# Transnormer attention and bilinear feed-forward on one core: batch 2's load ahead of w_out, batch 1's attention ahead of block 0's feed-forward, block 0's output product in pieces of two matmuls

## The chip, the cores and the metric

The kernel runs on one core of a Trainium2 chip. The metric is the device time of one execution in microseconds (us), the median of several runs. Profiles come from one profiled execution; their clock starts with the span, so a "time" in the text is the number of microseconds after the span's start. PE is the matrix engine (TensorE), DVE is VectorE, ACT is ScalarE, POOL is GpSimd and SP is SyncE. POOL and SP are used here to issue DMA transfers, ACT for a few.

## The reference

There are two parts, one after the other. The first is linear attention without a softmax, for 8 batches of 8 heads, 576 positions and a head width of 64. The second is a bilinear feed-forward on all 4608 tokens, with width 512 and inner width 1536.

```python
kv  = einsum('bhsd,bhse->bhde', k, v)            # 64 x 64 for each head
o   = einsum('bhsd,bhde->bhse', q, kv)
o   = o / sqrt(mean(o*o, axis=-1) + 1e-6) * g_norm
x   = o.transpose(0, 2, 1, 3).reshape(4608, 512) # heads side by side
out = ((x @ w_a) * (x @ w_b)) @ w_out
```

All inputs and the output are float32 in memory. The kernel casts to bf16 (attention) and f16 (feed-forward) as it loads.

## The kernel before, in words

**Attention.** The eight heads of a batch are handled as four pairs p, the 576 positions as two halves h of 288. For each of the eight (p, h) a chain runs: a PE product with the pair's kv matrix (`x_mm`, L344), ACT squares it (`sq_op`, L354), a PE product with a block of ones sums the squares (`s_mm`, L358), ACT makes the reciprocal root (`rs_op`, L362), and DVE scales the product by g and that root and writes it as f16 into `xp` (`xt_op`, L367), already transposed, as the right-hand side of the feed-forward. Both products of a chain take banks of a pool of three PSUM banks (rings `RQ` and `RS`, two each).

Batches 0 and 1 are loaded "early" with positions on partitions; PE transposes their q (L332) and makes their kv products in small matmuls (L316). They lie in tiles that are used for other things later (`abt`, `u`, `as`, `so`, `o_sb`, `c`, `T`). Batches 2 to 7 are loaded by `load_node`: POOL issues a copy of q into a scratch in DRAM (L562, two DMAs), k (L568, L569, five) and v (L574, L578, two), then SP issues one DMA that transposes the scratch into `qT` (L583). Their kv product is one group of 20 matmuls (L529). A load waits for the transpose of the load before it (`gate_t`, L559). k, v and qT have two buffers each.

**Feed-forward.** Tokens go in nine blocks of 512. Block 0 is done plainly (`std_block`, L378): for each of the 12 f-chunks, four matmuls with w_a and four with w_b, ACT copies the first result (L389) and DVE multiplies it by the second (L393) into `abt`. Its output product (`o_std`, L830) is four groups of 12 matmuls with w_out, ACT copies (L845), SP stores (L801).

Blocks 1 to 8 use Strassen's scheme in Winograd's form, with seven products in place of eight. Their x differences are four DVE operations for a block (L698), and each of six units j makes seven products of four matmuls of 256 columns (`wino_block`, L729). These are p1, p2, p6, p5, p7, p4 and p3, of which p1, p6, p7 and p4 accumulate in one bank X, with an ACT copy to `u` or `c` (L411) after each; p2 has a bank Y, and p5 and p3 share a bank Z. Three DVE additions (c11, c22, c12; L748) and one product (L783) end a unit. The weights need sums and differences of their own, made once by DVE: `weight_sums` (L638 of `four`, 16 operations, which can only change a weight in place when block 0 has read it) and `out_sums` for w_out (four operations, after block 0's output product has read it). The output product of blocks 1 to 8 is `o_unit` (L894), with DVE sums (L879), ACT copies (L926) and DVE additions (L932) and stores (L801); that of the last block is cut finer and uses two more banks W, so that the p4 products have banks of their own.

**What sets the order.** All operations are nodes of a `Plan`. Each has an engine, a duration, a priority number (lower goes first), dependencies and buffers that it takes and frees. `Plan.order()` simulates the engines and gives one fixed order; instructions are issued in that order on each engine, and semaphores keep the data right. Times of arrival of loaded data are written into it as constants (`W_AT`, `EARLY_AT`, `plan.at(46.5)` for w_out, and `issue_us`, `q_us`, `kv_us` in `load_node`). Priorities are times too: `at_win[b]` is the window over which a batch's attention is spread, `st[i]` the start of block i, `o_win` the window of an output product. The nodes of `load_node` go to POOL and SP; the early DMAs, with all weights, are issued before the plan's first node, in the order of the code. So the DMAs on POOL are: early batch 0, seven pieces of w_a and w_b each with batch 1's two halves between them, w_out in two halves (L296), and then batch 2 and the rest.

Of the kernel before, what the change touches and what calls it, by code (L numbers as in the profile page):

```python
# [135 lines left out]
def kernel(  # L136
# [11 lines left out]
    nc = tc.nc  # L148

    B, H, S, D = q.shape  # L150
    d_model = H * D
# [3 lines left out]
    FC = d_ff // 128  # L155
# [12 lines left out]
        [(5.2, 5.2, 6.0), (6.4, 7.0, 8.0), (7.6, 8.4, 9.2), (10.0, 10.8, 11.7)],  # L168
        [(19.0, 20.5, 22.0)] * 2 + [(28.8, 30.3, 31.8)] * 2,
    ]  # L170
    HP = H // 2
    R = 4 * S
    HM = d_ff // 2
# [2 lines left out]
    NMAX = N0 // 2  # L176
    nb = len(BLOCKS)
    NJ = FC // 2
    EH = d_model // 2

    const = ctx.enter_context(tc.tile_pool(name="const", bufs=1))
# [11 lines left out]
    wo_t = sb("wo_t", [128, FC, d_model], FP16)  # L193
# [53 lines left out]
    for p, homes in ((0, "woo"), (1, "ppc")):  # L247
        for n, src, eng, home in zip("qkv", (q, k, v), (nc.scalar, nc.sync, nc.sync), homes):
            t = carve(home, 2 * EC * D, FP32)[0:EP].rearrange("p (h c d) -> p h c d", h=2, d=D)
# [20 lines left out]
    for i in range(2):  # L270
        t = const.tile([128, NP, 128], BF16, name=f"kvd{i}")
# [14 lines left out]
    wo_v = moe_w_out.rearrange("(fc p) e -> p fc e", p=128)  # L286

    for i, (f0, f1) in enumerate(WB):
        sl = slice(f0, f1)
        nc.gpsimd.dma_start(out=wa_t[:, :, sl], in_=wa_v[:, :, sl])  # L290
        nc.gpsimd.dma_start(out=wb_t[:, :, sl], in_=wb_v[:, :, sl])
        if i in (2, 4):
            early_load(early[1], 1, slice((i // 2 - 1) * HP, i // 2 * HP))
    for i in range(2):
        sl = slice(i * FC // 2, (i + 1) * FC // 2)
        nc.gpsimd.dma_start(out=wo_t[:, sl, :], in_=wo_v[:, sl, :])  # L296


    def dummies(n):
# [97 lines left out]
    def mm_us(n, cols):  # L397
        return n * (cols / 2400 + 0.0025)
# [16 lines left out]
    plan = Plan({"PE": 5.7, "DVE": 3.3, "ACT": 2.7, "SP": 5.0, "POOL": 22.5, "V": 0.0})  # L415
# [96 lines left out]
    def late_batch(b, load, win):  # L512
        at = Attn(b)
        w0, w1 = win
        kb, vb, qb = load["k"], load["v"], load["q"]
        kd = Buf(RKD)
        at.qt = [qb, kd]

        def view(t):
            return t[:, 0 : H * (NCH + 1) * D].rearrange("p (h c d) -> p h c d", h=H, d=D)  # L520

        s = Buf(RS)

        def kv_mm():
            kv_ps = s.tile[:].rearrange("p (a e) -> p a e", a=NP)
            for c in range(NCH + 1):
                for p in range(NP):
                    hs = slice(2 * p, 2 * p + 2)
                    nc.tensor.matmul(  # L529
                        kv_ps[:, p, :],  # L530
                        lhsT=kb.tile[:, c, hs, :],
                        rhs=view(vb.tile)[:, hs, c, :],
                        start=(c == 0 and p == 0),
                        stop=(c == NCH and p == NP - 1),
                    )

        n = plan.add(
            "PE", 1.15, w0, kv_mm, [(load["n"], load["kv_us"]), plan.at(w0 - 3)], [s, kd], [kb, vb]
        )

        def kv_out():
            kv_ps = s.tile[:].rearrange("p (a e) -> p a e", a=NP)
            at.kvd = kd.tile
            nc.scalar.copy(at.kvd[0:D, :, 0:D], kv_ps[0:D, :, 0:D])
            nc.scalar.copy(at.kvd[D:, :, D:], kv_ps[D:, :, D:])
            for p in range(NP):
                at.q[p] = qb.tile[:, p, :]

        m = plan.add("ACT", 0.75, w0, kv_out, [n], (), [s])
        slices(at, (w0 + 0.12 * (w1 - w0), w1), lambda p: [m, (load["qn"], 5.5)])  # L550


    def load_node(b, prio, dep):
        ld = {"k": Buf(RK), "v": Buf(RV), "q": Buf(RQT)}
        scr = scr_pool.tile([NP, S, 2, D], BF16, name="scr", tag="scr")

        def issue():
            if dep is not None:
                nc.gpsimd.tensor_copy(gate_t, dep["q"].tile[0:1, 0, 0:1])  # L559
            qv = q[b].rearrange("(p hl) s d -> hl s p d", hl=2)  # L560
            for hl in range(2):
                nc.gpsimd.dma_start(  # L562
                    out=scr[:, :, hl, :].rearrange("p s d -> s p d"), in_=qv[hl]
                )
            kt = ld["k"].tile
            ks = k[b, :, 0:SA, :].rearrange("h (sp c) d -> sp h c d", c=NCH)
            for c in range(NCH):
                nc.gpsimd.dma_start(out=kt[:, c], in_=ks[:, :, c, :])  # L568
            nc.gpsimd.dma_start(out=kt[0:SB, NCH], in_=k[b, :, SA:S, :].rearrange("h sp d -> sp h d"))  # L569
            for n, src in (("v", v),):  # L570
                t = ld[n].tile[:, 0 : H * (NCH + 1) * D].rearrange(
                    "p (h c d) -> p h c d", h=H, d=D
                )
                nc.gpsimd.dma_start(  # L574
                    out=t[:, :, 0:NCH, :],
                    in_=src[b, :, 0:SA, :].rearrange("h (sp c) d -> sp h c d", c=NCH),
                )
                nc.gpsimd.dma_start(  # L578
                    out=t[0:SB, :, NCH, :], in_=src[b, :, SA:S, :].rearrange("h sp d -> sp h d")
                )  # L580

        def transpose():
            nc.sync.dma_start_transpose(  # L583
                out=ld["q"].tile[:].rearrange("p a s -> p (a s)"),
                in_=scr[:].rearrange("a s h d -> (a s) (h d)"),
            )

        issue_us, q_us, ld["kv_us"] = (18.0, 8.0, 18.0) if dep is None else (9.0, 1.5, 11.5)

        ld["n"] = plan.add(  # L590
            "POOL", issue_us, prio, issue, [(dep["qn"], 5.5)] if dep else [], [ld["k"], ld["v"]]
        )
        ld["qn"] = plan.add(
            "SP", 2.5, prio, transpose, [(ld["n"], q_us)], [ld["q"]]
        )
        return ld
# [70 lines left out]
    def out_sums(prio):  # L667
        add, sub = nc.vector.tensor_add, nc.vector.tensor_sub
        b11, b12 = wo_t[:, 0:NJ, 0:EH], wo_t[:, 0:NJ, EH:]
        b21, b22 = wo_t[:, NJ:, 0:EH], wo_t[:, NJ:, EH:]  # L670
        t2, t3, t4 = (so_t[:, i] for i in range(3))
        n3, n1, n2, n4 = four(
            prio,
            fast_us(NJ * EH),
            ((t3, b22, b12, sub), (b12, b12, b11, sub), (t2, b22, b12, sub), (t4, b21, t2, sub)),
            [plan.at(46.5)],
            list(o_reads),
        )
        return n1, n2, n3, n4
# [140 lines left out]
    def o_std(ab, muls, win):  # L820
        w0, w1 = win
        ob = Buf(ROS)
        ng, copied = N0 // 128, []
        for g in range(ng):
            pr = w0 + (w1 - w0) * g / ng
            ps = Buf((RO, RY)[g % 2])

            def mm(g=g, ps=ps):
                for fc in range(FC):
                    nc.tensor.matmul(  # L830
                        ps.tile[:],
                        lhsT=ab.tile[:, fc, g * 128 : (g + 1) * 128],
                        rhs=wo_t[:, fc, :],
                        start=(fc == 0),
                        stop=(fc == FC - 1),
                    )

            n1 = plan.add(
                "PE", mm_us(FC, d_model), pr, mm,
                [plan.at(46.5)] + list(muls.values()), [ps], [ab],  # L840
            )
            o_reads.append(n1)
            n2 = plan.add(
                "ACT", act_us(d_model), pr,
                lambda g=g, ps=ps: nc.scalar.copy(ob.tile[:, g], ps.tile[:]),  # L845
                [n1] + copied[-1:], [ob] if g == 0 else [], [ps],
            )
            copied.append(n2)
            plan.add(
                "SP", 0.45, pr + 1, lambda g=g: store(g * 128, ob.tile[:, g]), [n2], (), [ob]  # L850
            )

    def o_unit(r0, ab, muls, osum, pr, du, chunks, pieces, m, w, first, second, X, Y, Z, ob, s2, s3, s4, W):
        v = nc.vector
# [95 lines left out]
        n1, n2, n3, n4 = osum  # L950
        if W:
# [22 lines left out]
                c21 = comb(6 + 0.1 * i, 1, 0, W[i], [p4, e3], [W[i]], subs)  # L974
                put(1, subs, [c21, c22], queue=("ACT", "SP")[i])
            return
        p1 = prod(0, X, a11, b11, True, [plan.at(46.5)], [X])
        e1 = ev(0, 0, 0, p1, [ob])
        p2 = prod(1, Y, a12, b21, True, [], [Y])
        c11 = comb(1, 0, 0, Y, [p2, e1], [Y])  # L980
# [17 lines left out]
    st = [T0]  # L998
    for i in range(len(lens)):
        st.append(st[-1] + lens[i] + (o_us[i - 1] if i else 0) + late_us * n_at[i])  # L1000
    L = [st[i + 1] - st[i] for i in range(len(lens))]
    at_win = {1: (34.5, st[1] - 3)}
    for b in range(2, B):
        t = b * S / N0
        at_win[b] = (max(61.0, st[int(t) - 1] + (t % 1) * L[int(t) - 1] - 18), st[int(t)] - 22 + (t % 1) * 12)
    loads = {2: load_node(2, 22.5, None)}
    for b in range(3, B):
        loads[b] = load_node(b, at_win[b - 1][0], loads[b - 1])
    early_batch(0, (4.0, 16.0))
    early_batch(1, at_win[1])  # L1010
    ab, muls, reads = std_block((st[0], st[1]))
    wsum = weight_sums(32.5, reads)
    needs = {1: [], 2: [2], 3: [3], 4: [4], 5: [5], 6: [6], 7: [7], 8: []}
    O_A, O_B = 12.0, 3.0
    for bi in range(1, nb + 1):
        o_win = (st[bi] + 1.0, st[bi + 1] - 1.0) if bi < nb else (st[bi] + O_A, st[bi + 1] + O_B)
        if bi == 1:
            o_std(ab, muls, o_win)
            osum = out_sums(st[2] - 10)
        else:  # L1020
            o_block(bi - 1, ab, muls, osum, o_win, 2, (RO, RY, RY), 1)
        for b in needs[bi]:
            late_batch(b, loads[b], at_win[b])
        ab, muls = wino_block(bi, (st[bi], st[bi + 1]), wsum)
# [40 lines left out]
```

## Time and profile before

| | |
|---|---|
| median of 5 runs | 306.39 us (306.2 to 307.17) |
| profiled execution, its own time | 306.52 us |
| its span, first to last instruction | 304.7 us |
| mean granted PE clock | 0.987 |
| PE busy | 292.1 us, 96% of the span |
| DVE busy | 234.8 us, 77% |
| ACT busy | 192.9 us, 63% |
| POOL busy | 76.3 us, 25% |

The profiled execution has 1.8 us outside its span. Matmuls overlap in the profile: a matmul of 256 columns is shown as 273 ns long while the next starts 109 ns later, so PE's "busy" share is no measure of lost time, and the starts are the thing to read. The page's second part cuts the span into 40 slices of 7.6 us, with one digit for a tenth of busy time. In a timeline a row gives start, length, engine, line, operation, what is written from what, the shape, how many are merged, and in brackets the idle time before it and what ended it. A row of the waits gives who waited for whom, the total, the number of waits and the longest.

### The profile page before, as it was taken

To read this page: it belongs to the slowest core of one execution; us is meant where nothing else is said; L and a number is where in the kernel's file an instruction comes from. 1 tells how busy PE (TensorE), PEld (TensorE's weight loads), DVE (VectorE), ACT (ScalarE), POOL (GpSimd) and SP (SyncE) were. 2 spreads that over 40 slices of the span, in tenths; PEclk is the share of its full clock that TensorE was granted. 3 is DMA by queue.
4 is the path that set the end of the run, shared out by engine and by line. 5 is a ranking of instruction groups with operands and counts; after the bars stand their busy time and mean duration, and the time that the engine had idled before them with its cause. 6 is when DMAs were issued, how large, how long until landed. Compare 5 with 4: busy or idle time off the path is not lost.

```text
span 304.7 us, 6666 instructions
## 1 busy us (share of the span) xinstructions
PE 292.1 (96%) x2620; PEld 239.1 (78%) x2621; DVE 234.8 (77%) x433; ACT 192.9 (63%) x404; POOL 76.3 (25%) x93
## 2 busy tenths in 40 slices
PE   7699899999999999999999999999999999999992
PEld 2444445498788898888988898889888888888881
DVE  4343778569998979698969986998599849898652
ACT  3574456289897768875688548965797466655520
POOL 8665742092470831904700000000000000000000
PEclk9699999999999999999999999999999999999999
DMA  8999999999799899999964400030004001100123
GB/s 197 209 199 198 199 205 159 187 180 170 78 144 160 55 156 242 114 175 168 155 73 80 138 3 0 2 140 1 2 0 140 1 2 69 72 3 0 51 89 138
DMA packets 98815, 33.16 MB, mean 109 GB/s; under 512 B 76768, under 2 KB 94176, under 8 KB 98784
## 3 DMA queue, kind: packets, MB, share of 16 engines
q0 software_dynamic: 77984, 17.99, 63.2%
q1 hardware_dynamic: 20096, 13.64, 18.5%
q10 hardware_dynamic: 704, 1.11, 1.2%
q8 instruction: 20, 0.33, 0.4%
q14 instruction: 11, 0.09, 0.1%
HBM read 37.75 MB, written 12.98 MB: 166 GB/s over the span
## 4 chain that ended last, share of the span: by engine, by line
PE 90%; DVE 4%; DMA 3%; ACT 1%; SPq 0%; issue 0%; DVEq 0%
PE bk L729 47%; PE bk L894 24%; PE bk L378 7%; PE bk L830 3%; DMA c<-in_v_dram 3%; PE bk L358 3%; PE bk L344 2%; PE bk L529 2%; PE bk L316 1%; DVE c L748 1%; DVE o_sb L932 1%; PE bk L332 1%; ACT rs L362 0%; DVE abt L393 0%; DVE xp L367 0%; SPq L250 0%
## 5 line engine op out<-in xcount | busy, mean ns | idle before, releaser
L748 DVE TENSOR_TENSOR c<-bk,u 128x512 f16<-128x512 f32 x144 | 96.6, 685 | 27.2 <-PE bk L729 13.2
L411 ACT COPY u<-bk 128x512 f32<-128x512 f32 x144 | 82.2, 591 | 37.5 <-PE bk L729 36.4
L729 PE MATMUL bk<-xp,wa_t 128*128 128x256 f16 x288 | 55.0, 273 | 0.0
L729 PE MATMUL bk<-xp,wb_t 128*128 128x256 f16 x288 | 55.0, 273 | 0.0
L729 PEld LDWEIGHTS <-wa_t 128*128 128x128 f16 x384 | 37.4, 98 | 5.1
L367 DVE SCALAR_TENSOR_TENSOR xp<-bk,g_col,rs 128x288 f16<-128x288 f32 x64 | 32.5, 511 | 11.4 <-ACT rs L362 11.2
L894 PEld LDWEIGHTS <-abt 128*128 128x128 f16 x384 | 37.5, 98 | 4.8 <-DVE abt L783 0.2
L729 PEld LDWEIGHTS <-wb_t 128*128 128x128 f16 x384 | 37.6, 98 | 4.4
L411 ACT CAST c<-bk 128x512 f16<-128x512 f32 x48 | 28.3, 590 | 17.2 <-PE bk L729 16.6
L894 PE MATMUL bk<-wo_t,abt 128*128 128x256 f16 x288 | 37.0, 273 | 0.0
L729 PE MATMUL bk<-T,sa 128*128 128x256 f16 x192 | 36.6, 273 | 0.1
L729 PE MATMUL bk<-T,sb 128*128 128x256 f16 x192 | 36.6, 273 | 0.0
L362 ACT ACTIVATE rs<-bk,eps_t 128x288 f32<-128x288 f32 x64 | 32.4, 508 | 3.5 <-PE bk L358 3.2
L783 DVE TENSOR_TENSOR abt<-c 128x1024 f16<-128x1024 f16 x48 | 32.9, 685 | 1.7
L729 PEld LDWEIGHTS <-sa 128*128 128x128 f16 x288 | 28.1, 98 | 4.4 <-issue 0.7
L894 PEld LDWEIGHTS <-as 128*128 128x128 f16 x288 | 28.2, 98 | 3.4
L729 PEld LDWEIGHTS <-sb 128*128 128x128 f16 x288 | 28.2, 98 | 3.3
L354 ACT ACTIVATE sq<-bk 128x288 bf16<-128x288 f32 x64 | 25.5, 413 | 2.5 <-PE bk L344 2.3
L926 ACT COPY o_sb<-bk 128x512 f32<-128x512 f32 x31 | 18.2, 586 | 13.0 <-PE bk L894 12.3
L894 PE MATMUL bk<-so,as 128*128 128x256 f16 x192 | 25.7, 273 | 0.0
L568 POOL DMA_DIRECT2D k_t<-in_k_dram x24 | 21.2, 901 | 3.0 <-PE bk L529 2.6
L358 PE MATMUL bk<-sq,ones 128*128 128x288 bf16 x64 | 18.8, 293 | 2.3 <-ACT rs L362 1.3
(97 smaller groups left out, 396.3 us busy)
## 6 DMA issues: line engine op xcount, KB each, us to landing
out_dram<-o_sb SPq DMA_DIRECT2D x22, 256.0 KB, 2.3
scr<-in_q_dram POOLq DMA_DIRECT2D x12, 288.0 KB, 6.2
k_t<-in_k_dram POOLq DMA_DIRECT2D x24, 128.0 KB, 5.4
v_t<-in_v_dram POOLq DMA_DIRECT2D x6, 512.0 KB, 8.4
wo_t<-in_moe_w_out_dram POOLq DMA_DIRECT2D x2, 768.0 KB, 14.5
out_dram<-o_sb SPq DMA_DIRECT2D x12, 128.0 KB, 3.0
wa_t<-in_moe_w_a_dram POOLq DMA_DIRECT2D x5, 256.0 KB, 10.9
wb_t<-in_moe_w_b_dram POOLq DMA_DIRECT2D x5, 256.0 KB, 10.9
```

Of the source, the lines that this page charges most:

```text
L354: nc.scalar.activation(sq, self.x_ps[p, h][:, 0:HF], AF.Square)
L358: nc.tensor.matmul(ps[:, 0:HF], lhsT=ones, rhs=self.sq[p, h], start=True, stop=True)
L362: nc.scalar.activation(rs, self.s_ps[p, h][:, 0:HF], AF.Abs_reciprocal_sqrt, bias=eps_t)
L367: nc.vector.scalar_tensor_tensor(out=xcols(p, self.b * S + h * HF, HF), in0=self.x_ps[p, h][:, 0:HF], scalar=g_col, in1=self.rs[p, h], op0 ...
L378: nc.tensor.matmul(ps[:, 0:n], lhsT=w[:, kc, fc * 128 : (fc + 1) * 128], rhs=xcols(kc, 0, n), start=(kc == 0), stop=(kc == KC - 1),)
L411: ("ACT", act_us(n), lambda: nc.scalar.copy(*args())),
L568: nc.gpsimd.dma_start(out=kt[:, c], in_=ks[:, :, c, :])
L729: nc.tensor.matmul(ps.tile[:, i * n : (i + 1) * n], lhsT=lhs(w, sm)[:, kc, :], rhs=rhs()[:, kc, :], start=start and i == 0 and kc == 0, st ...
L748: lambda: nc.vector.tensor_add(cs(fi, h), full(ps), u.tile),
L783: nc.vector.tensor_mul(t, c[:, :, :, 0], c[:, :, :, 1])
L894: nc.tensor.matmul(ps.tile[:, sub * EH : (sub + 1) * EH], lhsT=lhs(slice(j, j + 1))[:, 0, sub * 128 : (sub + 1) * 128], rhs=rhs[:, j, :], ...
L926: lambda: nc.scalar.copy(o(fi, h), bank(X, every)), [dep], takes, frees,
```

## The change

Five things are done, all in the order of the work; no operation's arithmetic or shape is altered.

1. The two DMAs of w_out leave their place after the weights and are issued inside batch 2's `load_node`, after its k and v. The constants of arrival follow: w_out at 58.5 instead of 46.5 (`WO_AT`), batch 2's k and v and its transpose earlier, and q of a late batch 7.5 instead of 5.5 after its transpose was issued.
2. Batch 1's attention has the window 24 to 38 instead of 34.5 to three before the end of block 0.
3. Batch 2's attention may begin at 53 instead of 61.
4. `weight_sums` has priority 38 instead of 32.5, so that DVE prefers batch 1's attention.
5. Block 0's output product has its window 8 us later, and each of its four groups of 12 matmuls is planned as six nodes of two matmuls, each waiting only for its own two f-chunks, so that other work can stand between them.

```diff
--- before.py
+++ after.py
@@ -168,6 +168,7 @@
         [(5.2, 5.2, 6.0), (6.4, 7.0, 8.0), (7.6, 8.4, 9.2), (10.0, 10.8, 11.7)],
         [(19.0, 20.5, 22.0)] * 2 + [(28.8, 30.3, 31.8)] * 2,
     ]
+    WO_AT = 58.5
     HP = H // 2
     R = 4 * S
     HM = d_ff // 2
@@ -176,6 +177,7 @@
     NMAX = N0 // 2
     nb = len(BLOCKS)
     NJ = FC // 2
+    OP = 2
     EH = d_model // 2
 
     const = ctx.enter_context(tc.tile_pool(name="const", bufs=1))
@@ -291,9 +293,6 @@
         nc.gpsimd.dma_start(out=wb_t[:, :, sl], in_=wb_v[:, :, sl])
         if i in (2, 4):
             early_load(early[1], 1, slice((i // 2 - 1) * HP, i // 2 * HP))
-    for i in range(2):
-        sl = slice(i * FC // 2, (i + 1) * FC // 2)
-        nc.gpsimd.dma_start(out=wo_t[:, sl, :], in_=wo_v[:, sl, :])
 
 
     def dummies(n):
@@ -547,7 +546,7 @@
                 at.q[p] = qb.tile[:, p, :]
 
         m = plan.add("ACT", 0.75, w0, kv_out, [n], (), [s])
-        slices(at, (w0 + 0.12 * (w1 - w0), w1), lambda p: [m, (load["qn"], 5.5)])
+        slices(at, (w0 + 0.12 * (w1 - w0), w1), lambda p: [m, (load["qn"], 7.5)])
 
 
     def load_node(b, prio, dep):
@@ -578,6 +577,10 @@
                 nc.gpsimd.dma_start(
                     out=t[0:SB, :, NCH, :], in_=src[b, :, SA:S, :].rearrange("h sp d -> sp h d")
                 )
+            if dep is None:
+                for i in range(2):
+                    sl = slice(i * FC // 2, (i + 1) * FC // 2)
+                    nc.gpsimd.dma_start(out=wo_t[:, sl, :], in_=wo_v[:, sl, :])
 
         def transpose():
             nc.sync.dma_start_transpose(
@@ -585,10 +588,10 @@
                 in_=scr[:].rearrange("a s h d -> (a s) (h d)"),
             )
 
-        issue_us, q_us, ld["kv_us"] = (18.0, 8.0, 18.0) if dep is None else (9.0, 1.5, 11.5)
+        issue_us, q_us, ld["kv_us"] = (16.0, 6.0, 13.0) if dep is None else (9.0, 1.5, 11.5)
 
         ld["n"] = plan.add(
-            "POOL", issue_us, prio, issue, [(dep["qn"], 5.5)] if dep else [], [ld["k"], ld["v"]]
+            "POOL", issue_us, prio, issue, [(dep["qn"], 7.5)] if dep else [], [ld["k"], ld["v"]]
         )
         ld["qn"] = plan.add(
             "SP", 2.5, prio, transpose, [(ld["n"], q_us)], [ld["q"]]
@@ -673,7 +676,7 @@
             prio,
             fast_us(NJ * EH),
             ((t3, b22, b12, sub), (b12, b12, b11, sub), (t2, b22, b12, sub), (t4, b21, t2, sub)),
-            [plan.at(46.5)],
+            [plan.at(WO_AT)],
             list(o_reads),
         )
         return n1, n2, n3, n4
@@ -825,20 +828,24 @@
             pr = w0 + (w1 - w0) * g / ng
             ps = Buf((RO, RY)[g % 2])
 
-            def mm(g=g, ps=ps):
-                for fc in range(FC):
-                    nc.tensor.matmul(
-                        ps.tile[:],
-                        lhsT=ab.tile[:, fc, g * 128 : (g + 1) * 128],
-                        rhs=wo_t[:, fc, :],
-                        start=(fc == 0),
-                        stop=(fc == FC - 1),
-                    )
-
-            n1 = plan.add(
-                "PE", mm_us(FC, d_model), pr, mm,
-                [plan.at(46.5)] + list(muls.values()), [ps], [ab],
-            )
+            n1 = None
+            for f0 in range(0, FC, OP):
+
+                def mm(g=g, ps=ps, f0=f0):
+                    for fc in range(f0, f0 + OP):
+                        nc.tensor.matmul(
+                            ps.tile[:],
+                            lhsT=ab.tile[:, fc, g * 128 : (g + 1) * 128],
+                            rhs=wo_t[:, fc, :],
+                            start=(fc == 0),
+                            stop=(fc == FC - 1),
+                        )
+
+                n1 = plan.add(
+                    "PE", mm_us(OP, d_model), pr + 0.01 * f0, mm,
+                    [plan.at(WO_AT), n1] + [muls[fc] for fc in range(f0, f0 + OP)],
+                    [ps] if f0 == 0 else [], [ab],
+                )
             o_reads.append(n1)
             n2 = plan.add(
                 "ACT", act_us(d_model), pr,
@@ -974,7 +981,7 @@
                 c21 = comb(6 + 0.1 * i, 1, 0, W[i], [p4, e3], [W[i]], subs)
                 put(1, subs, [c21, c22], queue=("ACT", "SP")[i])
             return
-        p1 = prod(0, X, a11, b11, True, [plan.at(46.5)], [X])
+        p1 = prod(0, X, a11, b11, True, [plan.at(WO_AT)], [X])
         e1 = ev(0, 0, 0, p1, [ob])
         p2 = prod(1, Y, a12, b21, True, [], [Y])
         c11 = comb(1, 0, 0, Y, [p2, e1], [Y])
@@ -999,23 +1006,23 @@
     for i in range(len(lens)):
         st.append(st[-1] + lens[i] + (o_us[i - 1] if i else 0) + late_us * n_at[i])
     L = [st[i + 1] - st[i] for i in range(len(lens))]
-    at_win = {1: (34.5, st[1] - 3)}
+    at_win = {1: (24.0, 38.0)}
     for b in range(2, B):
         t = b * S / N0
-        at_win[b] = (max(61.0, st[int(t) - 1] + (t % 1) * L[int(t) - 1] - 18), st[int(t)] - 22 + (t % 1) * 12)
+        at_win[b] = (max(53.0, st[int(t) - 1] + (t % 1) * L[int(t) - 1] - 18), st[int(t)] - 22 + (t % 1) * 12)
     loads = {2: load_node(2, 22.5, None)}
     for b in range(3, B):
         loads[b] = load_node(b, at_win[b - 1][0], loads[b - 1])
     early_batch(0, (4.0, 16.0))
     early_batch(1, at_win[1])
     ab, muls, reads = std_block((st[0], st[1]))
-    wsum = weight_sums(32.5, reads)
+    wsum = weight_sums(38.0, reads)
     needs = {1: [], 2: [2], 3: [3], 4: [4], 5: [5], 6: [6], 7: [7], 8: []}
     O_A, O_B = 12.0, 3.0
     for bi in range(1, nb + 1):
         o_win = (st[bi] + 1.0, st[bi + 1] - 1.0) if bi < nb else (st[bi] + O_A, st[bi + 1] + O_B)
         if bi == 1:
-            o_std(ab, muls, o_win)
+            o_std(ab, muls, (o_win[0] + 8.0, o_win[1] + 8.0))
             osum = out_sums(st[2] - 10)
         else:
             o_block(bi - 1, ab, muls, osum, o_win, 2, (RO, RY, RY), 1)
```

## The prediction

> **What bounds the kernel now.** First the page: busy shares, slices, the chain that ended last.
>
> ```profile
> PE 292.1 (96%) x2620; PEld 239.1 (78%) x2621; DVE 234.8 (77%) x433; ACT 192.9 (63%) x404; POOL 76.3 (25%) x93
> ...
> PE   7699899999999999999999999999999999999992
> ...
> DMA  8999999999799899999964400030004001100123
> ...
> PE 90%; DVE 4%; DMA 3%; ACT 1%; SPq 0%; issue 0%; DVEq 0%
> ```
>
> TensorE (PE) is the bound: 90% of the chain. The row of 9s hides small losses, so I counted them. The trace gives the spacing of PE starts: 0.216 us for a 512-column matmul (12 in 2.59), 0.109 for 256, 0.123 for 288, 0.056 for 128, about 0.04 for the small transposes and head products. Against that, from the first L378 (19.66) to batch 2's product L529 (62.84) PE had 40.77 us of work in 43.18: 2.41 lost. From there to batch 3's L529 (80.72) 0.37 is lost, to batch 4's (109.62) 0.47, and from batch 4's to batch 7's (205.32) nothing. So **3.25 us** are lost after 20 us, all before 110. Next, who PE waited for between 20 and 300 us:
>
> ```profile
> PE bk L358 <- ACT rs L362: 1.3, 2, 0.7
> PE bk L358 <- ACT kvd L326: 0.6, 1, 0.6
> PE bk L316 <- DVE c L339: 0.3, 1, 0.3
> PE bk L729 <- DVE c L748: 0.2, 1, 0.2
> ```
>
> And where, in PE's timeline:
>
> ```profile
> 36.86 0.28 PE L358 MATMUL bk<-sq,ones 128*128 128x288 bf16 x1 [0.65 <-ACT kvd L326]
> 37.73 0.28 PE L358 MATMUL bk<-sq,ones 128*128 128x288 bf16 x1 [0.59 <-ACT rs L362]
> ...
> 49.50 0.28 PE L358 MATMUL bk<-sq,ones 128*128 128x288 bf16 x1 [0.69 <-ACT rs L362]
> 49.62 2.75 PE L830 MATMUL bk<-wo_t,abt 128*128 128x512 f16 x12
> ...
> 62.84 1.28 PE L529 MATMUL bk<-v_t,k_t 128*128 128x128 bf16 x20
> ```
>
> The large waits are all L358, the sum-of-squares product of batch 1's attention: two of its chains (PE, ACT, PE, ACT, DVE) run with nothing of block 0 put between them.
>
> The other resource is the load queue on POOL, busy until 60 us:
>
> ```profile
> 30.17 0.82 POOL L296 DMA_DIRECT2D wo_t<-in_moe_w_out_dram  x1 [0.60 <-DMA wb_t<-in_moe_w_b_dram]
> 31.65 0.82 POOL L296 DMA_DIRECT2D wo_t<-in_moe_w_out_dram  x1 [0.66 <-DMA abt<-in_q_dram]
> 33.08 1.65 POOL L562 DMA_DIRECT2D scr<-in_q_dram  x1 [0.61 <-DMA abt<-in_k_dram]
> ...
> 61.04 0.51 POOL L559 COPY gate_t<-qT 1x1 bf16<-1x1 bf16 x1 [10.81 <-DMA qT<-scr]
> ```
>
> Each issue starts about 0.28 us after the landing of the DMA eight before it (30.17 after 29.89), with some 10 us of transfers always ahead. Landings: last weight piece 39.72, w_out 43.52 and 47.36, batch 2's q copy 51.15, k 55.03, v 59.76; its transpose ran 51.22 to 60.99.
>
> Last, the end:
>
> ```profile
> 297.54 1.47 PE L894 MATMUL bk<-wo_t,as 128*128 128x256 f16 x12
> 297.74 0.59 ACT L926 COPY o_sb<-bk 128x512 f32<-128x512 f32 x1 [1.16 <-PE bk L894]
> 298.36 0.69 DVE L932 TENSOR_TENSOR o_sb<-bk,u 128x512 f32<-128x512 f32 x1 [3.80 <-ACT o_sb L926]
> 298.97 1.34 DVE L932 TENSOR_TENSOR o_sb<-bk,o_sb 128x256 f32<-128x256 f32 x3
> 299.47 1.25 ACTq L801 DMA_DIRECT2D out_dram<-o_sb  x2
> ```
>
> The last matmul starts at 298.74. Four DVE adds follow one another to 300.3, and the last two of four 256 KB stores go out together at 300.34 and land at 303.40 and 303.61.
>
> **What the Trainium skill says.** "TensorE: Matmul & The Clock Gate", What happens when you issue a matmul: "The MATMULs themselves stay in program order". So a matmul waiting for w_out or for a DVE result holds all behind it; the trace has them in the written order. Its section Back-to-back issue gap gives N/2.4 + 2.5 ns, 109 ns for 256 columns and 216 for 512; it calls this the isolated gap, yet the full stream here runs at exactly that. "DMA: Bandwidth & Descriptors", Queues, rings and completion order: each DMA engine takes turns between the queues it has work for. So SP's transpose shares engines with POOL's loads; here k and v took 8.6 us beside it (51.15 to 59.76).
>
> **The change part by part.** The order in which the changed kernel's instructions stand has the same 48 + 96 matmuls of 512 columns and the same others; PE's work is 286.5 us either way. No compute is removed, so all that can move is waits.
>
> *Batch 1's attention earlier.* Its pieces now stand between block 0's matmuls from f-chunk 1 on. Is the data there? Heads 0 to 3 landed at 21.60 (q), 23.06, 24.54; the transposes would now run at 22.8 and 25.6, the products at 26.0. Heads 4 to 7: 31.37, 32.80, 34.38, used at 33.2 and 36.0. Weights of chunks 4, 5: 35.71, 37.08, used at 39. I followed each of the eight chains with ACT at 0.41 (square) and 0.51 (rs) and DVE at 0.51: every result is ready 0.1 to 1 us before PE reaches its user. So the first 27 us lose about nothing: 96 x 0.216 + 17 x 0.123 + 96 small = 26.9, and block 1 starts at 46.56 (47.52 before, with a part of the attention still to come and then 0.69 of wait).
>
> *Block 1 ahead of the output product.* Before, L830 (10.4 us of PE without much DVE) covered the second half of the weight sums. Now 19 products of block 1 (76 x 0.109 = 8.3) come first, and DVE must deliver. Its queue from 44.4: two x differences (0.46 each), block 0's product (0.61), two differences and two sums (0.33 to 0.47 each), the last product (0.61) to 48.2, two in-place sums of 0.47 to 49.15, then the first c11 (0.69) to 49.84. That releases the bank of the second p2, which PE reaches at 49.61: 0.3 lost. Two sums and c22 end at 51.4: p3 loses 0.23. Two sums and c12 end at 52.9: the next p5 loses 0.22. Then DVE needs 2.4 us (three adds, one product) of every 3.06 on PE and keeps up. **New loss 0.8**; bounds 0 (DVE somewhat earlier) and 3.8 (all eight late sums of 0.47 on the path). I take the walk.
>
> *Batch 2 ahead of w_out.* Nine DMAs move ahead of two on POOL; bytes are the same, so the queue still empties near 59.8. q lands near 43.5, k 47.4, v 52.1, w_out 56 and 59.8. The transpose, first on SP, starts at 43.6 and takes 9.8 (as here) to 11.6 (the longest of the six in the trace): 53.4 to 55.2. Users: L529 at 55.7, q at 59.0, w_out's first half at 62.7, second at 64.0. All covered, by 3 to 6 us. The gate of batch 3 opens some 7 us earlier, but its loads stand behind w_out and land near 64 to 73. On SP its transpose now stands behind two stores, so it starts near 67 and ends near 77; PE wants it at 82. Batch 5's stands behind block 1's stores (near 118), ends near 130; wanted after 145. No cost.
>
> *Output product in pieces of two, 8 us later.* The same 48 matmuls. The first 24 are still nearly in one run, the rest stand between block 1's products, so DVE gets 2.6 us per group while attention of batch 2 (eight of 0.51) is due. The output sums (four of 0.96) move to near 81 and block the adds for 3 us; by the same walk their users come 0.6 to 1.2 us later. I put 0.4 of loss between 56 and 110 in place of 0.84; bounds 0 and 1.5.
>
> So batch 4's L529 starts at 19.66 + 86.71 + 0.8 + 0.4 = 107.6 instead of 109.62: **2.05 gained**.
>
> *The end.* In the new order p3 stands ahead of the two p4 halves, p4's second half is last, and the square-size add after it is 256 wide. From the last matmul's start: 0.27 to finish, 0.41 for the add, 0.09 around them, so the last store goes out 0.77 after instead of 1.60, alone instead of as a pair (2.1 to 2.5 us to land against 3.1 to 3.3). Gain 0.8 (issue only) to 1.4; I take **1.1**.
>
> Sum 3.15 against the profiled execution: 306.52 (span 304.7, 1.8 outside it) gives 303.4. The median of the runs is 0.13 lower: **303.2**.
>
> **The rivals.**
> 1. *DVE takes it back* in block 1: the loss at 46 to 56 is 2 to 3.8 rather than 0.8. For it: DVE is 11.75 busy of 14 us at 36 to 50 already. Against: it is idle 4.5 of 11 us at 50 to 61, and the walk above leaves it behind PE only three times. Time 304.4 to 306.2.
> 2. *w_out late, slower.* If the transpose held the engines instead of sharing them, its 9.8 us would add to the queue: w_out lands at 69.6, PE stands at the output product 5.6 us, 308.8. It decides from a landing at 67.2 on. Against it: 8.6 us of k and v went by beside a transpose.
> 3. *The pieces don't interleave*: 24 of 48 do not. Then the loss at 56 to 110 stays 0.84: 303.6.
>
> **How the numbers follow.** The forecast with rival 3 has 0.73, rival 1 0.16, rival 2 and other lost cover (SP's order) 0.11. A measurement of this kernel can tell about 0.2% (0.6 us) from no change; rival 1's slow end gives most of "same". Low end: no new loss and a full gain at the end, 3.25 + 1.4 off, 301.8. High end: well into rival 1, 305.4.
>
> **What would show it.** Right: waits of L358 gone; block 1 starts near 46.6; L529 of batches 2, 3, 4 near 55.7, 79.4, 107.6; waits of the block 1 products (L729's place) for DVE at 49 to 53 of some 0.8; no wait for w_out; the last store some 0.8 after the last matmul. Wrong: a wait of the output product for a DMA, DVE waits over 2 us in block 1, or new waits after 110.

## The result, and the profile after

The changed kernel is slower: 307.88 us median against 306.46 for the kernel before, ratio 1.0045 with a 95% interval of 1.0032 to 1.0057. The profiled execution took 307.85 us (span 305.8). The forecast was 303.2 us. The changed kernel also scatters more: its fast runs go from 305.8 to 309.8 us (one slow run, at 310.84, is left out of the ratio), while nearly all runs of the kernel before lie within 305.6 to 307.2. Lines of the changed kernel are named by its own numbers: L343, L357, L528, L732, L836, L901 and L939 were L344, L358, L529, L729, L830, L894 and L932.

From the page of the changed kernel, the busy shares, the slices and the chain:

```profile
PE 292.4 (96%) x2620; PEld 239.7 (78%) x2621; DVE 236.5 (77%) x433; ACT 194.3 (64%) x404; POOL 76.4 (25%) x93
...
PE   6699999699999999999999999999999999999993
...
PEclk9789999979999999999999999999999999999999
DMA  8999999999999799899993400030004000300043
...
PE 78%; DMA 18%; POOL 1%; issue 1%; DVE 0%; SPq 0%; POOLq 0%
```

The 8 in the slice at 30 to 38 us of the kernel before is gone from PE's row, but the slice at 53 to 61 us shows 6, and the clock row shows 7 in the slice after it. DMA has 18% of the chain instead of 3%. The waits of PE between 20 and 300 us are one line:

```profile
PE bk L343 <- DMA qT<-scr: 3.2, 1, 3.2
```

None of the waits of L358 in the profile before is left. In their place PE stands still once, for batch 2's transposed q (`qT`), which `x_mm` needs. PE's timeline there (start, length, idle before it in brackets):

```profile
58.06 0.38 PE L732 MATMUL bk<-T,wa_t 128*128 128x256 f16 x2
58.27 0.38 PE L732 MATMUL bk<-T,wb_t 128*128 128x256 f16 x2
61.87 0.56 PE L343 MATMUL bk<-qT,kvd 128*128 128x288 bf16 x2 [3.21 <-DMA qT<-scr]
62.22 0.64 PE L732 MATMUL bk<-xp,wa_t 128*128 128x256 f16 x2
62.65 0.63 PE L732 MATMUL bk<-xp,wb_t 128*128 128x256 f16 x2
```

Before the wait two pairs of 256-column matmuls start 0.21 us apart; after it they start 0.43 us apart, until 65.4. Busy time by stretch says the same (the columns are PE, weight loads, DVE, ACT and POOL, then the granted clock, the DMA share and GB/s):

```profile
50.00:58.60 8.60, 8.47 (x85) 7.23 (x83) 6.98 (x13) 5.67 (x12) 0.00 (x0) 1.00 1.18 174
58.60:61.80 3.20, 0.06 (x1) 0.00 (x0) 0.56 (x1) 0.72 (x2) 0.00 (x0) 1.00 0.99 158
61.80:65.40 3.60, 3.53 (x17) 2.51 (x17) 1.81 (x3) 1.08 (x3) 3.15 (x3) 0.53 0.24 22
```

The granted clock is 0.53 over the 3.6 us after the standstill. Counted as in the prediction, from batch 2's L528 (55.19) to batch 3's (83.72) PE had 23.51 us of work and took 28.53: **5.0 us lost, 3.4 by the wait and 1.6 to 1.7 by the slow clock after it**. What PE waited for is the transpose; here it is in SP's queue and in the answer on the tile qT, whose last line is the time from issue to landing:

```profile
43.41 7.90 SPq L586 DMA_TRANSPOSE qT<-scr  x1
```

```profile
L586 SPq DMA_TRANSPOSE qT<-scr x1: 7902/7902/7902, 43.4 to 43.4; - x1
...
  PE bk L343: 3.2, 1
...
DMA to landing us min/median/max: 18.4/18.4/18.4
```

It was issued when expected, 43.41, and landed at 61.83: 18.4 us, where the kernel before took 9.8. In both its first packet came 4.1 to 4.2 us after the issue (47.57, and 55.35 after 51.22), so what got longer is the flow of its 2336 packets: 14.3 us instead of 5.6. At the end of the kernel, the stores:

```profile
299.96 1.51 DVE L939 TENSOR_TENSOR o_sb<-bk,o_sb 128x512 f32<-128x512 f32 x3
300.68 0.86 ACTq L804 DMA_DIRECT2D out_dram<-o_sb  x2
```

The last matmul starts at 300.74 and the last store lands at 304.78, so 4.04 after it; before, 298.74 and 303.61, 4.87.

### The profile page after: what moved, and what is told of

Same layout as the page of the kernel before. It is cut to its first block, busy times and chain, and to the rows that moved or that the text cites. A ratio compares the mean times of both kernels' runs of the same rounds, so it can differ in the third digit from the quotient of the medians.

```text
span 305.8 us, 6675 instructions
## 1 busy us (share of the span) xinstructions
PE 292.4 (96%) x2620; PEld 239.7 (78%) x2621; DVE 236.5 (77%) x433; ACT 194.3 (64%) x404; POOL 76.4 (25%) x93
## 3 DMA queue, kind: packets, MB, share of 16 engines
q0 software_dynamic: 77984, 17.99, 63.1%
## 4 chain that ended last, share of the span: by engine, by line
PE 78%; DMA 18%; POOL 1%; issue 1%; DVE 0%; SPq 0%; POOLq 0%
PE bk L732 45%; PE bk L901 24%; DMA qT<-scr 6%; DMA scr<-in_q_dram 4%; DMA wb_t<-in_moe_w_b_dram 4%; PE bk L836 3%; DMA as<-in_k_dram 3%; DMA wa_t<-in_moe_w_a_dram 2%; PE bk L343 2%; PE bk L357 2%; PE bk L528 2%; POOL scr L561 1%; POOL wb_t L293 0%; POOL so L238 0%; DVE o_sb L939 0%
## 5 line engine op out<-in xcount | busy, mean ns | idle before, releaser
L732 PE MATMUL bk<-xp,wa_t 128*128 128x256 f16 x288 | 55.2, 274 | 0.1
L732 PE MATMUL bk<-xp,wb_t 128*128 128x256 f16 x288 | 55.2, 274 | 0.0
L732 PEld LDWEIGHTS <-wa_t 128*128 128x128 f16 x384 | 37.6, 98 | 6.3 <-issue 0.4
L732 PEld LDWEIGHTS <-wb_t 128*128 128x128 f16 x384 | 37.8, 98 | 4.6
L901 PEld LDWEIGHTS <-abt 128*128 128x128 f16 x384 | 37.5, 98 | 4.6
L901 PE MATMUL bk<-wo_t,abt 128*128 128x256 f16 x288 | 37.0, 273 | 0.0
L732 PE MATMUL bk<-T,sb 128*128 128x256 f16 x192 | 36.6, 273 | 0.0
L732 PE MATMUL bk<-T,sa 128*128 128x256 f16 x192 | 36.6, 273 | 0.0
L732 PEld LDWEIGHTS <-sa 128*128 128x128 f16 x288 | 28.3, 99 | 4.9 <-issue 0.2
L732 PEld LDWEIGHTS <-sb 128*128 128x128 f16 x288 | 28.3, 98 | 3.5
L901 PEld LDWEIGHTS <-as 128*128 128x128 f16 x288 | 28.2, 98 | 3.5
L901 PE MATMUL bk<-so,as 128*128 128x256 f16 x192 | 25.7, 273 | 0.0
L933 ACT COPY o_sb<-bk 128x512 f32<-128x512 f32 x31 | 18.2, 586 | 10.6 <-PE bk L901 9.9
L561 POOL DMA_DIRECT2D scr<-in_q_dram x12 | 19.6, 1637 | 2.0 <-issue 1.4
```

The costliest lines, as they stand in the source:

```text
L561: nc.gpsimd.dma_start(out=scr[:, :, hl, :].rearrange("p s d -> s p d"), in_=qv[hl])
L732: nc.tensor.matmul(ps.tile[:, i * n : (i + 1) * n], lhsT=lhs(w, sm)[:, kc, :], rhs=rhs()[:, kc, :], start=start and i == 0 and kc == 0, st ...
L901: nc.tensor.matmul(ps.tile[:, sub * EH : (sub + 1) * EH], lhsT=lhs(slice(j, j + 1))[:, 0, sub * 128 : (sub + 1) * 128], rhs=rhs[:, j, :], ...
L933: lambda: nc.scalar.copy(o(fi, h), bank(X, every)), [dep], takes, frees,
```

## The experiments

Times are medians; each ratio is to the kernel before, run again beside the experiment (306.25, 306.55 and 306.39 us in three groups of runs). Diffs are shortened to the lines that matter, and lines in a view have the numbers of the kernel that it shows. Three theories are tested. Theory A: w_out's long packets beside it stretch the transpose. Theory B: it is stretched because it starts earlier, beside k and v and a full POOL queue. Theory C: the slow stretch after the wait is a clock taken back while PE stood still.

**w_out behind the transpose.**

```diff
 def issue():
     if dep is not None:
         nc.gpsimd.tensor_copy(gate_t, dep["q"].tile[0:1, 0, 0:1])
+    if b == 3:
+        for i in range(2):
+            sl = slice(i * FC // 2, (i + 1) * FC // 2)
+            nc.gpsimd.dma_start(out=wo_t[:, sl, :], in_=wo_v[:, sl, :])
...
-    if dep is None:
-        for i in range(2):
-            sl = slice(i * FC // 2, (i + 1) * FC // 2)
-            nc.gpsimd.dma_start(out=wo_t[:, sl, :], in_=wo_v[:, sl, :])
```

> The changed kernel with its instruction order on PE, DVE and ACT untouched; only w_out's two DMAs are issued later, at the head of batch 3's load, after the gate that waits for batch 2's transpose. Theory A (the transpose is stretched by w_out's long packets beside it): the transpose, 18.4 us in the changed kernel, takes 9.8 to 11.6, lands near 54, PE's wait of 3.2 us for qT is gone; w_out then lands near 60 and 64, and PE may wait up to 1 us for its second half. About 303.5 us. Theory B (it is stretched because it starts earlier, beside k and v and a full POOL queue): it still takes 15 us or more, the wait for qT stays, and w_out comes at 70: over 312 us.

Measured 307.41 us, ratio 1.0025 (1.0010 to 1.0040). The transpose, issued at 43.55, took 10.1 us. It started when it does in the changed kernel, beside the same k and v, so theory B falls as far as these go; POOL's queue is shorter here, by w_out, and the next run keeps it full. In the DMA view of 50 to 54 us only v's last packets still stand beside it:

```profile
q1 hardware_dynamic: 1819, 0.46, 92.0%
q0 software_dynamic: 213, 0.03, 10.6%
```

(queue 1 is SP's transpose, queue 0 POOL's loads; packets, MB, share.) But the time is 4 us above the expected 303.5: w_out's second half landed at 66.41, not 64, and PE stood still there instead, again with a slow clock behind it (0.50 at 66.6 to 69.9).

```profile
66.45 1.41 PE L836 MATMUL bk<-wo_t,abt 128*128 128x512 f16 x3 [3.37 <-DMA wo_t<-in_moe_w_out_dram]
```

**w_out in half rows.**

```diff
-    nc.gpsimd.dma_start(out=wo_t[:, sl, :], in_=wo_v[:, sl, :])
+    for e in (slice(0, EH), slice(EH, d_model)):
+        nc.gpsimd.dma_start(out=wo_t[:, sl, e], in_=wo_v[:, sl, e])
```

> The changed kernel, w_out loaded as four DMAs of half rows (256 columns) in place of two of whole rows, so that its packets are 512 B in place of 1024 B; same bytes, same order on PE, DVE and ACT. Theory A in its exact form (an engine gives one packet to each queue in turn, so the transpose's speed is set by the length of the other queue's packets: 155 transpose packets a us beside 1024 B ones): about 270 a us, the transpose lands near 57.5, before PE wants it at 58.7; no wait for qT; w_out's end stays near 63. About 303 us. Theory B (start time or k and v), or a sharing by bytes: the transpose still lands at 61 or later, 307 to 308 us.

Measured **302.52 us**, ratio 0.9882 (0.9866 to 0.9898). The transpose took 14.3 us and landed at 58.05; PE's first product with it started at 58.09, and PE waited for nothing between 20 and 300 us. The instructions on PE stand in the changed kernel's order, so the late transpose is the whole loss. Here POOL's queue is as full as in the changed kernel, and theory B had the transpose landing at 61 or later, so what was left of it falls too. The packets of both queues, first in the changed kernel at 52 to 60 us, then here at 52 to 57:

```profile
q0 software_dynamic: 1225, 1.23, 91.6%
q1 hardware_dynamic: 1223, 0.31, 31.7%
```

```profile
q0 software_dynamic: 1212, 0.61, 87.8%
q1 hardware_dynamic: 1211, 0.31, 46.5%
```

One packet for one, in both. Beside packets of 1024 B the transpose gets 153 of its 256 B packets a us, beside 512 B 242. In these two views the queues share by the count of packets and not by bytes, and the length of w_out's packet sets the pace: some 96 ns for 1024 B and 58 ns for 512 B (the share times 16 engines and the time, over the packets).

**w_out in quarter rows.**

```diff
-    nc.gpsimd.dma_start(out=wo_t[:, sl, :], in_=wo_v[:, sl, :])
+    for e0 in range(0, d_model, 128):
+        e = slice(e0, e0 + 128)
+        nc.gpsimd.dma_start(out=wo_t[:, sl, e], in_=wo_v[:, sl, e])
```

> The changed kernel with w_out as eight DMAs of quarter rows (128 columns, packets of 256 B). One packet for one: the transpose goes on speeding up (153 packets a us beside 1024 B, 242 beside 512 B, over 300 here) and lands near 56, but w_out's own rate falls and its last quarter may land after 64, when PE wants it: 302.5 us if it comes in time, 304 to 308 with a wait of the output product for w_out. If the transpose has a floor of its own near 14 us, it lands at 58 again.

Measured 302.46 us, ratio 0.9872 (0.9849 to 0.9895): not to be told from half rows. The transpose landed at 56.18, 13.2 us after its issue, so it went on getting shorter; at 52 to 54 its packets came at about 336 a us, again one for one:

```profile
q0 software_dynamic: 674, 0.17, 82.8%
q1 hardware_dynamic: 671, 0.17, 64.4%
```

w_out's last quarter landed at 62.80, and PE stood still for 0.4 us before the output product's second half (62.89).

**PE kept busy in the wait.**

```diff
 def x_mm(self, p, h, ps):
+    if self.b == 2 and not self.x_ps:
+        for _ in range(15):
+            nc.tensor.matmul(
+                banks[4][:], lhsT=wa_t[:, 0, 0:128], rhs=wa_t[:, 0, 0:512], start=True, stop=True
+            )
```

> The changed kernel with 15 matmuls of 512 columns that nothing reads, put on PE just ahead of batch 2's first product with qT, where PE stands still for 3.2 us. Theory C (of the 5.0 us lost at 58 to 66, 1.7 are a slower PE clock after the standstill: 16 matmuls of 256 columns with starts 214 ns apart instead of 109): with PE kept busy the slow stretch is gone, batch 3's L528 comes near 82.0 instead of 83.7 and the time is about 306.2. Against it (the slow stretch comes from something else at that place, such as the weight loads): nothing changes, 307.9, or it gets slower by what the dummies overrun.

Measured 306.07 us, ratio 0.9996 (0.9984 to 1.0008). The transpose landed at 61.77, as late as in the changed kernel, but the stretch behind it ran at full clock:

```profile
58.60:61.80 3.20, 2.97 (x14) 1.27 (x13) 0.24 (x1) 0.40 (x1) 0.00 (x0) 1.00 1.01 163
61.80:65.40 3.60, 3.59 (x33) 3.15 (x33) 2.53 (x5) 2.52 (x6) 3.20 (x3) 1.00 0.25 20
```

33 matmuls in the 3.6 us where the changed kernel had 17, and batch 3's L528 at 82.01. Theory C holds: counted from PE's first product with qT to batch 3's L528 it is 20.2 us instead of 21.9, so 1.7 us were the clock. "TensorE: Matmul & The Clock Gate" of the Trainium skill, What's actually happening, says that PE falls to half its clock after an idle window of about 3.4 us and needs a busy one to come back; here 3.2 us of standstill with a clock of 0.53 over 3.6 us agrees in kind, and so does the wait of 1.8 us in the kernel with all but the load order (below), after which the clock stayed at 1.00 (82 to 90 us).

**Batch 2's attention planned behind the transpose.**

```diff
-    slices(..., lambda p: [m, (load["qn"], 7.5)])
+    slices(..., lambda p: [m, (load["qn"], 16.0 if b == 2 else 7.5)])
```

> The changed kernel with one constant of the plan altered: batch 2's products with qT are planned 16 us after the transpose's issue, not 7.5, so they stand some 8 us later in PE's order, behind block 0's first output products; the DMAs stay as they are. If the late transpose is the whole loss and the rest of the prediction holds: the transpose still takes 18 us and lands near 61.8, PE doesn't wait for it, w_out's second half at 63.0 is just in time, about 303 us. If the loss is elsewhere, or if moving these products opens another wait: 305 to 308 us.

Measured 303.01 us, ratio 0.9903 (0.9879 to 0.9927). The transpose took 18.2 us as before and PE did not wait for it. This shows by a second way that the wait is the loss: the DMAs are the changed kernel's own, and only the order of the work on the engines is another.

**Half rows and a later attention together** (the same line with 12.5 in place of 16.0).

> The changed kernel with w_out in half rows and batch 2's products with qT planned 12.5 us after the transpose's issue in place of 7.5, so PE wants qT near 62.5 and it lands near 58. In the run with half rows alone qT landed 0.04 us before PE wanted it, so this one should be as fast with 4 us to spare: 302.2 to 302.8 us, and no wait for qT or w_out. If the later attention crowds DVE at 80 to 90 as in the run with the attention after the transpose: 303.0.

Measured 303.08 us, ratio 0.9898 (0.9883 to 0.9913). That is above the 302.2 to 302.8 expected. PE waits for neither qT nor w_out; its last matmul starts 0.45 us later than with half rows alone (295.80 against 295.35), 0.31 of it already at the start of block 1. The two are not to be told apart.

**The parts alone.** Batch 1's attention alone (with the priority of the weight sums, which belongs to it), on the kernel before:

```diff
-at_win = {1: (34.5, st[1] - 3)}
+at_win = {1: (24.0, 38.0)}
-wsum = weight_sums(32.5, reads)
+wsum = weight_sums(38.0, reads)
```

> The kernel before, with batch 1's attention earlier (window 24 to 38) and the priority of the weight sums at 38, and nothing else of the change. By the prediction's first step: block 1 starts near 46 instead of 47.5, the three waits of L358 at 36 to 50 are gone, and the new order ends with p4 last, which is worth 0.8 us at the end. If that step carries the gain alone: about 303.5 us, and the other parts are not needed. If its gain is given back, because block 1 and block 0's output product then crowd on DVE: 305 to 306.5 us.

Measured 303.97 us, ratio 0.9913 (0.9898 to 0.9928). Block 1 starts at 45.84 and the last store lands 4.05 us after the last matmul. Some of the gain is given back at 76 to 82: counted by the starts of PE's matmuls, some 2.2 us in six places. The two that the view marks as waits are:

```profile
79.25 0.38 PE L729 MATMUL bk<-xp,sa 128*128 128x256 f16 x2 [0.32 <-DVE c L748]
81.57 0.38 PE L729 MATMUL bk<-xp,wa_t 128*128 128x256 f16 x2 [0.48 <-DVE xp L367]
```

All but the load order: w_out's DMAs ahead of batch 2's load again, with the arrival constants of before (46.5, and 18, 8, 18 in `load_node`).

> The changed kernel with w_out issued ahead of batch 2 again and the plan's times of arrival for both as before; early attention and pieces of two stay. The transpose then has no w_out beside it and takes about 9.8 us (51 to 61). If the order of the loads was never needed: about 303 us, no wait for qT or w_out. If batch 2's attention so late (qT at 61) opens waits at 60 to 80: 304 to 306 us.

Measured 304.14 us, ratio 0.9917 (0.9890 to 0.9944). The transpose took 9.8 us (51.63 to 61.40). A wait for batch 3's x differences comes at 82, so the old load order does leave something. (The four runs go from 303.06 to 304.89 us, and the profiled one is the slowest.)

```profile
82.25 0.39 PE L731 MATMUL bk<-xp,wa_t 128*128 128x256 f16 x2 [1.82 <-DVE xp L700]
```

The pieces of two alone, on the kernel before (the diff of `o_std` and its window as in the change, w_out still at 46.5):

> The kernel before with block 0's output product in pieces of two matmuls and its window 8 us later, and nothing else of the change. The waits of L358 at 36 to 50 belong to batch 1's attention and stay in part, p3 stays last at the end; the pieces can fill the wait at 49.5 (0.7 us) and the losses at 60 to 110 (0.8 us). Expected 305 to 306 us. If the pieces do nothing: 306.3.

Measured 306.97 us, ratio 1.0020 (1.0014 to 1.0027). A gain was expected; they cost 0.6 us. The waits of L358 at 36 to 50 stay, 0.7 us are lost at 77 instead of 0.4, and batch 4's L529 comes at 110.03 instead of 109.62.

Half rows on the kernel before (the same edit as above, at L296):

> The kernel before, with w_out loaded as four DMAs of half rows, as in the run of the changed kernel with half rows. Here w_out has landed before the transpose starts, so if half rows helped there by letting the transpose through, nothing changes here: 306.2 us, transpose 9.8 us. If half rows are a faster load in themselves, w_out lands before 47.4 and the time falls below 305.5.

Measured 306.58 us, ratio 1.0002 (0.9992 to 1.0011). w_out landed at 47.65 and the transpose took 9.8 us, so half rows are worth nothing where no transpose runs beside w_out. Their 5 us in the changed kernel are the transpose's.

## Why the prediction was wrong, step by step

**The step that failed** is one sentence in *Batch 2 ahead of w_out*: "The transpose, first on SP, starts at 43.6 and takes 9.8 (as here) to 11.6 (the longest of the six in the trace)". It started at 43.4 and took 18.4, so it landed at 61.8 and not at 53.4 to 55.2, and PE wanted it at 58.5. The six transposes of the profile before had run beside copies of q, k and v, or beside nothing. I took their spread for the bound, though none had w_out beside it; the trace before does not show this case, so the range of 9.8 to 11.6 had no measurement behind its upper end. The prediction even named the mechanism, the turns that a DMA engine takes between its queues, and cited it ("DMA: Bandwidth & Descriptors", Queues, rings and completion order, which says that this happens packet by packet). It did not ask how long a turn of the other queue is. The runs show it: one packet of w_out, some 96 ns long for 1024 B, for every packet of the transpose of some 33 ns. At 153 a us the last 1441 of its 2336 packets, from 52 us on, need 9.4 us. In the kernel before, POOL's queue had little to put beside the transpose, 908 packets at 55 to 61 us, with 275 B in the mean (v's):

```profile
q0 software_dynamic: 908, 0.25, 40.3%
```

The spread of six was no safe bound without w_out either: with all but the load order, a later transpose (issued at 112.91) took 16.7 us with no packet of w_out beside it. PE did not wait for that one, and its cause was not looked for.

Rival 2 had the right place, the shared DMA engines, and the wrong victim: I let the transpose hold up w_out. That its time, 308.8 us, lies near the measured 307.9 is chance. The cover given for qT, landing at 55.2 at the latest against use at 59.0, was 6.6 us too large by the landing.

**The price of a standstill** was missing too: rival 2 puts its wait of 5.6 us at 5.6 us. The wait of 3.4 us (by starts) cost 5.0, since the clock was taken back. That alone makes the difference between "no change" (306.07 with PE kept busy) and slower.

The other steps, by their own numbers:

- *Batch 1's attention earlier*: right. The waits of L358 are gone; block 1 starts at 46.20 (forecast 46.56). Alone it is worth 2.6 us, 0.8 of them at the end.
- *Block 1 ahead of the output product*: right in place and size. From block 1's start to batch 2's L528 8.99 us for 8.31 of work, 0.68 lost against 0.8, at 49.45, 50.99 and 52.52.
- *Batch 2 ahead of w_out*: wrong for the transpose. k landed as forecast (47.15 for 47.4), v 1.8 us later (53.86) and w_out's halves 3.0 and 3.2 us later (58.98 and 62.97 for 56 and 59.8). That no product waited for w_out was partly luck: with half rows, where PE doesn't stand still, the second half landed at 62.32 and was wanted near 63.1, so 0.7 us were left of the forecast 4.2. The gate of batch 3 opened at 61.88, not 7 us earlier than before. The order itself looks worth having once the packets are short: 302.52 (half rows) and 302.46 us (quarter rows) with it, 304.14 without, four runs each; the intervals of the ratios overlap only a little (0.9866 to 0.9898 and 0.9849 to 0.9895 against 0.9890 to 0.9944).
- *Pieces of two*: I put 0.4 us of loss at 56 to 110 in place of 0.84. Apart from the wait and the clock the changed kernel loses nothing there after batch 3's product (27.96 us for 27.99 of work). But the pieces alone cost 0.6 us, so this gain comes from the order as a whole; which part of it brings the gain was not separated.
- *The end*: 0.83 us gained for a forecast 1.1. Direction and mechanism right; the last two stores still went out within 0.4 us of each other. The gain comes with batch 1's earlier attention (4.05 us from the last matmul to the last landing with it alone, 4.87 with the pieces alone).

With the one fault taken away and no other instruction moved on PE, the same steps give 302.52 us, 0.7 below the forecast. That it is below is not the prediction's merit: block 1 began at 45.62 there instead of 46.56, and at 46.20 in the changed kernel with the same instructions on PE.

## What to carry to other kernels

When a transfer is moved next to another one, compare packet lengths and not only bytes. Here the two queues moved one packet for one, so a transpose with 256 B packets crawled beside a load with 1024 B ones, and cutting the load into shorter rows gave the transpose its speed at no cost to the load (it landed at 62.32 and 62.80 instead of 62.97). A duration from the profile holds for the neighbours it had there. And a long wait of PE has a second price: the wait of 3.4 us cost half as much again through the clock, while one of 1.8 us did not. Such a wait is worth filling with other matmuls.

## What the runs showed of the hardware that was not expected

- Two DMA queues moved packet for packet: 1225 to 1223, 1212 to 1211, 674 to 671, with the packets of w_out's queue at 1024, 512 and 256 B and the transpose's at 256 B. The same transpose took 18.4, 14.3 and 13.2 us, and 10.1 with no w_out beside it.
- After 3.2 us of standstill PE ran at a granted clock of 0.53 for 3.6 us; with 15 unread matmuls in the gap it stayed at 1.00.
- What makes the changed kernel's time scatter over 4 us, and that of the kernel with w_out behind the transpose over 3.3 us, is settled only in part. Both have a standstill of over 3 us and a slow clock after it; the experiments without one scatter by 2 us or less. The changed kernel's runs fall into groups by their mean granted clock: 3 at 0.985 to 0.986 (median 305.9 us), 13 at 0.980 to 0.982 (307.6) and 12 at 0.975 to 0.977 (308.5). A stretch of 3.4 us at half the clock, as measured at 62.0 to 65.4, lowers the mean over 306 us by 0.0056, about the step from group to group. So the number of such stretches seems to differ from run to run; where they lie in runs without a profile is not shown.
